# A recurrent attention with hash-routed experts: another order of TensorE's groups in a tick, readers of the scores swapped, decay checks and last rows moved

## Chip, cores and metric

The kernel runs on one core of a Trainium2 chip. The metric is device time in microseconds (us). A run gives one time; the profile comes from one execution of its own, whose time is given beside its span.

## What is computed

A state of 40x40 per batch and head is updated for 768 time steps (RWKV-7), in 32 independent batch-head pairs; each of the 3072 output rows (4 batches x 768 steps, 8 heads x 40 = 320 wide) then goes through one of 8 experts, chosen by a hash of its token id.

```python
for t in range(S):                      # B, H, S, D = 4, 8, 768, 40
    y[:, :, t] = einsum('bhd,bhde->bhe', rt, state)
    Sa = einsum('bhde,bhe->bhd', state, at)
    state = state * wt[:, :, None, :] - einsum('bhd,bhe->bhde', Sa, bt)
    state = state + einsum('bhd,bhe->bhde', vt, kt)
...
expert_idx = token_ids * 2654435761 % 8
out[mask] = maximum(x[mask] @ w1[e], 0) @ w2[e]      # 320 -> 1024 -> 320
```

## The kernel before

**Attention.** The 768 steps are cut into 12 chunks of 64 and the 4 batches into 2 pairs: 24 tiles (`NU`), each with 2 batches x 8 heads. Inside a chunk the recurrence becomes products of 64x64 matrices per head, with running products of the decays multiplied into a, b, k and out of r and y. A tile passes through these groups of matmuls on TensorE (PSUM tile in brackets):

- `at_t` (t_ps, L472) and `z` (z_ps, L437): transposes of the scaled a (`at`) and of the scaled b and k (`z`), copied out by ScalarE; `at` and `z` are made by VectorE (L422, L424).
- `a` (a_ps): the scores of a with k and b. VectorE masks the k part into `mk` (L455); ScalarE copies the b part into `pk` (L463, L465) and `no` (L466). VectorE and ScalarE read the same PSUM tile, one after the other, in the order in which the program has them.
- After four tiles VectorE inverts their 32x32 blocks: a transpose `nb` (L494), 31 pairs of `outer` and `ub` (L503, L506) spread over 3.2 ticks, and two transposes `ut`, `ug` (L514, L515).
- `x` and `u` (x_ps, u_ps): the rest of the inverse `um` from those blocks, by way of `xi` (ScalarE, L533, L536, L546).
- `r0` and `r1` (both into r1_ps): a times the state, then mk times v; ScalarE copies the sum into `r1` (L606).
- `c` (c_ps and nc_ps): C, in two layouts, copied by ScalarE into `c_t` (L625, one copy per head parity) and into `x` (L629). Between the 40 columns of one head and the next, `x`, `z` and other ring buffers hold zeroed gaps up to 64.
- `v_t`, `r_t` (v_ps, t_ps), `rc` (rc_ps): products of r with C and v, masked by VectorE into `mr` (L642).
- `s` (s_ps): the next state, `st` (VectorE, L660); `sd` (sd_ps): its transposes.
- `y` (y_ps): the output, scaled by VectorE into `xs` (L675) and stored to `x_rows` in HBM by POOL (L679).

These groups are put into "ticks". Tile u enters at tick u with `at_t`, `z`, `a`; its `x`, `u`, `r0`, `r_t`, `v_t` come at tick u+7, its `r1`, `c`, `rc`, `s` at u+8 (`LAG` = 8), its `y` and `sd` at u+9. So ticks 0 to 7 hold only the first groups, ticks 8 to 23 all of them, ticks 24 to 32 only the later ones. Inside a tick the order is that of the list `STEPS` (L273), each group at the fraction index/14; work without a step (loads, the pairs of outer and ub, the decays, the routing) has ticks of its own. The whole list, sorted by tick, is issued in that order on TensorE, VectorE, ScalarE and POOL (`manual_schedule`), and each engine works through its own in order. SP's queue is placed by the framework.

The PSUM tiles of two banks (`two_banks`, L203) share three buffers, so each group waits for the readers of an earlier one. `at_t`, `r_t`, `x`, `u`, `s` use another pool of two single banks.

**Decays.** Six rounds (`decays`, L292), each for two chunks, load w (L311), check with two Relu activations that all decays lie in 0.65 to 1.5 (L318, sums into `wbad`), and form running products on VectorE: `pb` (L323, L330), `qb` (L335), and so on to two stores `p_rows`, `q_rows` by SP (L303), which POOL reads back as `pl`, `ql` (L409, L410). If a check fails, slow loops at the end redo the work; with these inputs they do not run.

**Experts.** For each of 8 experts: indirect gathers of its rows by POOL (L865), transposes and copies (`columns_of`), `up` (L891, L896: two batches of four PSUM banks, Relu alternating between ScalarE and VectorE), and `down` (L909) in tiles of 128 rows, copied out by ScalarE (L913) and scattered by POOL (L914). The weights of expert 0 come early; those of 1 and 2 by POOL, the others by SP.

Of the kernel before, what the change touches and what calls it, by code (L numbers as in the profile page):

```python
# [43 lines left out]
def kernel(  # L44
# [13 lines left out]
    nc = tc.nc  # L58
# [43 lines left out]
    nc.vector.memset(ones[:], 1.0)  # L102


    wbad = route.tile([P, 4 * S * B * H // (C * P)], F32)


    FH = F // 2
# [60 lines left out]
        return t  # L169

    at_r, r_r = (ring(n, 2, [P, HP, P], gaps) for n in ("at", "r"))
    x_r = ring("x", 3, [P, 2, HP, P], gaps2)
    z_r = ring("z", LAG + 2, [P, 2, HP, R], gap)

# [95 lines left out]
    plan = []  # L270


    STEPS = ["r1", "v_t", "at_t", "z", "c", "y", "r_t", "sd", "a", "rc", "r0", "x", "s", "u"]  # L273

    def at_tick(tick, step=None, order=0):
        if step is not None:
# [5 lines left out]
        return add  # L282

    rounds = [dict() for _ in range(NR)]
    lim = hold.tile([P, 2], F32, name="lim")
    nc.vector.memset(lim[:, 0:1], LO)
    nc.vector.memset(lim[:, 1:2], -HI)
    SEG = 4
    HC = C // 2
    SL = HC // SEG  # L290
# [1 line left out]
    def decays(ri, t0, span, t_f, span_f):  # L292

        x = rounds[ri]
        todo, then = [], []

        def segs(t):
            return t[:, 0:HC * D].rearrange("p (s t e) -> p s t e", s=SEG, e=D)


        def store(i, src):
            for y in range(2 * RN):
                nc.sync.dma_start(pq_dram[ri][i][y * HC:(y + 1) * HC].rearrange("t bh e -> bh t e"),  # L303
                                  src[y * BH:(y + 1) * BH].rearrange("p (t e) -> p t e", e=D))

        @at_tick(t0 - 1.0)
        def _():
            x["qb"] = qb = early.tile([P, (HC + 1) * D], F32, tag="qb", name="qb")
            for y in range(2 * RN):
                src = w.rearrange("b h (n t) e -> (b h) n (t e)", t=HC)[:, ri * 2 * RN + y]  # L310
                nc.sync.dma_start(qb[y * BH:(y + 1) * BH, 0:HC * D], src)  # L311

        @todo.append
        def _():
            x["pb"] = pb = early.tile([P, (HC + 1) * D], F32, tag="pb", name="pb")[:, 0:HC * D]

            for i, (sign, at) in enumerate(((-1.0, LO), (1.0, HI))):
                nc.scalar.activation(pb, x["qb"][:, 0:HC * D], AF.Relu, bias=lim[:, i:i + 1], scale=sign,  # L318
                                     accum_out=wbad[:, 2 * ri + i:2 * ri + i + 1])

        @todo.append
        def _():
            nc.vector.memset(segs(x["pb"])[:, :, 0, :], 1.0)  # L323


        for i in range(1, SL):
            @todo.append
            def _(i=i):
                p = segs(x["pb"])
                nc.vector.tensor_tensor(p[:, :, i], p[:, :, i - 1], segs(x["qb"])[:, :, i - 1], op=OP.mult)  # L330
        for i in range(SL - 2, -1, -1):
            @todo.append
            def _(i=i):
                q = segs(x["qb"])
                nc.vector.tensor_tensor(q[:, :, i], q[:, :, i], q[:, :, i + 1], op=OP.mult)  # L335

        @todo.append
        def _():

            q = segs(x["qb"])  # L340
            x["own"] = own = work.tile([P, SEG, D], F32, tag="own", name="own", bufs=1)
            nc.vector.tensor_copy(own[:, SEG - 1], q[:, SEG - 1, 0])
            for s in range(SEG - 2, -1, -1):
                nc.vector.tensor_tensor(own[:, s], q[:, s, 0], own[:, s + 1], op=OP.mult)  # L344

        @then.append
        def _():
            x["f_ps"] = p = bank([P, D], "f_ps")
            nc.tensor.matmul(p, lhsT=partner[:], rhs=x["own"][:, 0], start=True, stop=True)  # L349

        @then.append
        def _():

            x["ends"] = ends = work.tile([P, SEG + 1, D], F32, tag="ends", name="ends", bufs=1)
            nc.vector.tensor_scalar(ends[:, SEG], x.pop("f_ps"), second[:, 0:1], None, op0=OP.add)
            nc.vector.tensor_tensor(ends[:, 0:SEG], x["own"][:],
                                    ends[:, SEG].unsqueeze(1).to_broadcast([P, SEG, D]), op=OP.mult)
            x["rends"] = rends = work.tile([P, SEG, D], F32, tag="rends", name="rends", bufs=1)
            nc.vector.reciprocal(rends[:], ends[:, 0:SEG])

        @then.append
        def _():

            p = segs(x["pb"])
            nc.vector.tensor_tensor(p, p, x["rends"][:].unsqueeze(2).to_broadcast([P, SEG, SL, D]), op=OP.mult)
            store(0, x["pb"])

        @then.append
        def _():
            q = segs(x["qb"])  # L370
            nc.vector.tensor_tensor(q, q, x["ends"][:, 1:].unsqueeze(2).to_broadcast([P, SEG, SL, D]),
                                    op=OP.mult)
            nc.vector.tensor_copy(x["qb"][:, HC * D:], x["ends"][:, SEG])
            store(1, x["qb"][:, D:])

        @then.append
        def _():

            p = bank([P, P], "en_ps")
            nc.tensor.transpose(p[0:D], x["ends"][:, 0], ident[:])  # L380
            t = pend_r(ri)
            for par in range(2):
                for rn in range(RN):
                    src = p[0:D, rn * 2 * BH:rn * 2 * BH + BH].rearrange("p (b hp two) -> p two hp b", hp=HP, two=2)
                    nc.scalar.copy(t[half40(par), :, rn, :], src[:, par])

        for i, f in enumerate(todo):
            at_tick(t0 + span * i / len(todo), order=8)(f)
        for i, f in enumerate(then):
            at_tick(t_f + span_f * i / len(then), order=8)(f)  # L390
# [4 lines left out]
    def tile_a(u):  # L395
# [17 lines left out]
            load(lambda be, rows: by_head(kb[:, be], rows), b, 2 * g, n * C)  # L413
            load(lambda be, rows: by_head(kb[:, be], rows), k, 2 * g, n * C, crossed=True)

        @at_tick(u - 0.6)
        def _():
            x["at"], x["z"] = at_r(u), z_r(u)

            def view(t):  # L420
                return t.rearrange("p (hp two e) -> p hp two e", hp=HP, two=2)
            nc.vector.scalar_tensor_tensor(wide(x["at"]), by_head(x["a"]), -1.0, by_head(x["p"]), op0=OP.mult, op1=OP.mult)  # L422
            for be in range(2):
                nc.vector.tensor_tensor(heads(x["z"][:, be]), view(x["kb"][:, be]), view(x["q"][:, be]), op=OP.mult)  # L424
# [17 lines left out]
        def _():  # L442
            gi, ti = divmod(u, GRP)
            p = two_banks("a_ps")
            for kb in range(2):
                order = ("hq", "al", "be", "par") if kb == 0 else ("hq", "be", "al", "par")
                for par, be, hp in heads_by(*order):
# [3 lines left out]
                       x["at_t"][half40(par), hp, be, :])  # L451
            scores = p[:].rearrange("p two (kb hp t) -> p two kb hp t", kb=2, t=C)
            of_b = scores[:, :, 1]
            x["mk"] = mk = work.tile([P, 2, HP, C], F32, tag="mk", name="mk", bufs=LAG)
            nc.vector.tensor_tensor(mk[:], scores[:, :, 0], after[:].unsqueeze(1).unsqueeze(1).to_broadcast([P, 2, HP, C]),  # L455
                                    op=OP.mult)

            if ti == 0:
                groups[gi]["pk"] = (early.tile([P, GRP * H * BLK], F32, tag="pk", name="pk")[:]
# [4 lines left out]
            for i in range(2):  # L464
                nc.scalar.copy(pk[low(i)], of_b[low(i), :, :, BLK:C])  # L465
            nc.scalar.copy(no[:], of_b[:, :, :, BLK:C])  # L466

    def turn(t, src):

# [113 lines left out]
    def tile_b(u, t0):  # L583
# [14 lines left out]
        def _():  # L598
            p = x.pop("r1_ps")

            for par, _, hp in heads_by("hq", "par", "al"):
                c0 = hp % HQ * 2 * D
                mm(p[half(al(hp)), par, c0:c0 + 2 * D], x["mk"][:, par, hp, :], x["x"][:, :, hp, par * C:par * C + D],
                   start=False)
            x["r1"] = r1 = work.tile([P, 2, HQ, 2, D], F32, tag="r1", name="r1")
            nc.scalar.copy(r1[:].rearrange("p two q b e -> p two (q b e)"), p[:, :, 0:HP * D])  # L606

        @at_tick(t0, "c")
        def _():
# [3 lines left out]
            for par, be, hp in heads_by("hq", "be", "al", "par"):  # L613
                h, a = hx(par, be, hp), al(hp)
                c0 = (be * HQ + hp % HQ) * C
                mm(p[half40(par), a, c0:c0 + C], r1[half(a), par, hp % HQ, be, :], um[half(a), h, :])
            if not last:
                q = two_banks("nc_ps")
                for par, be, hp in heads_by("hq", "par", "al", "be"):
                    h, a = hx(par, be, hp), al(hp)  # L620
                    c0 = (hp % HQ * 2 + par) * D
                    mm(q[half(be), a, c0:c0 + D], um[half(a), h, :], r1[half(a), par, hp % HQ, be, :])
            x["c_t"] = ct = work.tile([P, 2, HP, C], F32, tag="c_t", name="c_t", bufs=1)
            for par in range(2):
                nc.scalar.copy(ct[half40(par)].rearrange("p b (a q) t -> p a b (q t)", a=2),  # L625
                               p[half40(par), :, 0:HP * C].rearrange("p a (b x) -> p a b x", b=2))
            if not last:
                for be in range(2):
                    nc.scalar.copy(x["x"][half(be), be].rearrange("p (a q) (two e) -> p a (q two) e", a=2, two=2)[:, :, :, 0:D],  # L629
# [33 lines left out]
        def _():  # L663
# [12 lines left out]
                                    by_parity(x["py"]), op=OP.mult)  # L676
            for be in range(2):
                r0 = (2 * g + be) * S + n * C
                nc.gpsimd.dma_start(x_rows[r0:r0 + C, :], xs[half(be), :])  # L679

        if not last:
            @at_tick(t0 + 1, "sd")
# [266 lines left out]
    def columns_of(e, xgs):  # L949
# [11 lines left out]
            nc.vector.tensor_copy(xt[:, :, TPE * P:], others[0][:])  # L961
        return xt

    others = [None]
    with tc.manual_schedule(engines={ET.PE, ET.DVE, ET.Activation, ET.Pool}):
        xt = columns_of(0, rows_of(0))
        weights(1, moe_w1[1], moe_w2[1], nc.gpsimd.dma_start)
        for e in range(E):
            xgs = rows_of(e + 1) if e + 1 < E else None
            if e == 0:  # L970
                weights(2, moe_w1[2], moe_w2[2], nc.gpsimd.dma_start)
            ht = mwork.tile([P, FP, SLOTS], F32, tag="ht", name="ht")
            up(xt, w1s[e], ht, SLOTS)
            if xgs is None:
                rest()
            else:
                xt = columns_of(e + 1, xgs)
# [119 lines left out]
```

## Time and profile before

| what | us |
|---|---|
| median of 3 runs | 800.42 (799.39 to 804.31) |
| the profiled execution | 798.8 |
| its span, first to last instruction | 797.0 |
| mean granted clock of TensorE | 0.853 of full speed |
| TensorE busy | 630.0 (79%) |
| VectorE busy | 373.5 (47%) |
| ScalarE busy | 281.7 (35%) |
| POOL busy | 227.7 (29%) |

Busy times are those of instructions alone, without what issues DMAs. Line numbers are those of the kernel before. "Idle before" in a row is the engine's own idle time ahead of that instruction, and the arrow names what ended it.

### The profile page before, as it was taken

How to read it: one execution, taken by the hardware profiler on the slowest of the kernel's cores; microseconds unless marked ns; L12 is line 12 of the kernel's file. 1: busy time of each engine (PE TensorE's matmuls, PEld its weight loads, DVE VectorE, ACT ScalarE, POOL GpSimd, SP SyncE). 2: the span in 40 equal slices, each digit the busy share in tenths (PEclk: the TensorE clock that was granted, in tenths of full speed). 3: DMA queues.
4: the chain of work that ended last, by engine and by line, in shares of the span. 5: the costliest groups of instructions: out<-in, count | busy, mean ns of one | idle time of the engine just before them, and what ended most of it. 6: DMA issues, size and time to landing. Idle time of an engine off the chain costs nothing.

```text
span 797.0 us, 25924 instructions
## 1 busy us (share of the span) xinstructions
PE 630.0 (79%) x11272; PEld 466.4 (59%) x11272; DVE 373.5 (47%) x925; ACT 281.7 (35%) x630; POOL 227.7 (29%) x381
## 2 busy tenths in 40 slices
PE   0025356788979788887997989569999999999995
PEld 0024345677867677776876777536565565664653
DVE  7062899977865796445647823122112022120210
ACT  2024325566554664554665565101101011100110
POOL 3222134123343453343332322171220311312101
PEclk9996655688676996886889999569999999999998
DMA  5939696574699587766343432282234125323000
GB/s 99 168 75 182 107 186 129 102 152 93 100 135 134 92 134 120 104 129 110 62 57 71 94 78 47 84 244 86 54 108 134 58 91 175 103 84 103 25 4 25
DMA packets 204918, 82.43 MB, mean 103 GB/s; under 512 B 186622, under 2 KB 195839, under 8 KB 204800
## 3 DMA queue, kind: packets, MB, share of 16 engines
q1 hardware_dynamic: 193088, 47.27, 31.6%
q0 software_dynamic: 11712, 33.46, 18.2%
q8 instruction: 90, 1.47, 0.8%
q14 instruction: 28, 0.23, 0.1%
HBM read 64.92 MB, written 16.42 MB: 102 GB/s over the span
## 4 chain that ended last, share of the span: by engine, by line
PE 55%; issue 17%; DVE 13%; ACT 5%; DMA 4%; SPq 3%; POOL 2%; POOLq 0%; DVEq 0%; ACTq 0%
PE dn_ps L909 9%; PE up_ps L891 9%; PE y_ps L247 5%; PE s_ps L247 4%; PE r_ps L247 4%; PE rc_ps L247 3%; PE t_ps L472 3%; PE a_ps L247 2%; PE u_ps L247 2%; PE z_ps L437 2%; PE up_ps L896 2%; PE sd_ps L687 2%; PE x_ps L247 2%; DVE outer L503 2%; DVE ub L506 2%
## 5 line engine op out<-in xcount | busy, mean ns | idle before, releaser
L899 DVE TENSOR_SCALAR ht<-up_ps 128x448 f32<-128x448 f32 x32 | 20.0, 625 | 196.1 <-PE up_ps L896 130.2
L909 PE MATMUL dn_ps<-w,ht 128*128 128x320 f32 (+1 forms) x448 | 109.5, 433 | 0.0
L909 PEld LDWEIGHTS dn_ps<-w,ht 128*128 128x128 f32 (+1 forms) x448 | 72.0, 177 | 32.1 <-issue 1.3
L891 PE MATMUL up_ps<-xt,w 128*128 128x448 f32 x224 | 87.5, 544 | 0.0
L914 POOL DMA_INDIRECT out_dram<-o,idx_all x28 | 27.6, 987 | 197.9 <-ACT o L913 179.8
L891 PEld LDWEIGHTS up_ps<-xt,w 128*128 128x128 f32 x224 | 41.7, 190 | 43.1 <-issue 37.9
L506 DVE TENSOR_TENSOR ub<-ub,outer 128x31 f32<-128x31 f32 (+15 forms) x186 | 63.8, 343 | 6.4
L901 ACT ACTIVATE ht<-up_ps 128x448 f32<-128x448 f32 x32 | 17.4, 545 | 136.1 <-PE up_ps L896 101.7
L679 POOL DMA_DIRECT2D x_rows<-xs x48 | 25.4, 534 | 138.0 <-DVE xs L675 62.1
L503 DVE TENSOR_TENSOR outer<-ub,nb 128x31 f32<-128x31 f32 (+15 forms) x186 | 62.7, 337 | 3.2
L913 ACT COPY o<-dn_ps 128x320 f32<-128x320 f32 x28 | 11.9, 426 | 119.4 <-PE dn_ps L909 119.4
L247 PE MATMUL a_ps<-at_t,z_t 40*64 40x64 f32 x1536 | 37.6, 250 | 20.4 <-ACT z_t L439 13.2
L558 POOL MEMSET x<- 64x512 f32 x48 | 25.0, 520 | 94.2 <-PE s_ps L247 92.9
L247 PEld LDWEIGHTS a_ps<-at_t,z_t 40*64 40x64 f32 x1536 | 32.5, 158 | 27.9 <-ACT z_t L439 17.1
L409 POOL DMA_DIRECT2D pl<-p_rows x48 | 25.6, 534 | 78.2 <-DVE at L422 52.0
L349 PE MATMUL f_ps<-own,partner 128*128 128x40 f32 x12 | 3.8, 404 | 53.6 <-DVE own L344 53.4
L675 DVE TENSOR_TENSOR xs<-y_ps,py 128x320 f32<-128x320 f32 x24 | 11.8, 491 | 70.7 <-PE y_ps L247 64.9
L437 PE MATMUL z_ps<-ident,z 128*104 128x128 f32 x192 | 39.3, 373 | 1.2 <-DVE z L424 1.2
L463 ACT COPY pk<-a_ps 128x256 f32<-128x256 f32 x24 | 8.9, 373 | 82.6 <-DVE mk L455 78.9
L472 PE MATMUL t_ps<-ident,at 128*104 128x128 f32 x96 | 23.9, 398 | 16.3 <-DVE at L422 16.2
L437 PEld LDWEIGHTS z_ps<-ident,z 128*104 128x104 f32 x192 | 34.5, 186 | 2.4 <-issue 1.2
L349 PEld LDWEIGHTS f_ps<-own,partner 128*128 128x128 f32 x12 | 2.9, 290 | 54.6 <-DVE own L344 53.9
(179 smaller groups left out, 1302.2 us busy)
## 6 DMA issues: line engine op xcount, KB each, us to landing
ql<-q_rows POOLq DMA_DIRECT2D x48, 160.0 KB
w<-in_moe_w_dram SPq DMA_DIRECT2D x10, 640.0 KB
w<-in_moe_w_dram SPq DMA_DIRECT2D x10, 512.0 KB
qb<-in_w_dram SPq DMA_DIRECT2D x24, 160.0 KB
al<-in_a_dram SPq DMA_DIRECT2D x48, 80.0 KB
kb<-in_b_dram SPq DMA_DIRECT2D x48, 80.0 KB
kb<-in_k_dram SPq DMA_DIRECT2D x48, 80.0 KB
r<-in_r_dram SPq DMA_DIRECT2D x48, 80.0 KB
```

The costliest lines, as they stand in the source:

```text
L247: nc.tensor.matmul(out_, lhsT=lhsT, rhs=rhs, start=start, stop=stop, skip_group_check=True)
L409: nc.gpsimd.dma_start(pl[half(be)], of_batches(p_rows, 2 * g + be, 1))
L437: nc.tensor.transpose(p[0:R, be, hp * P:(hp + 1) * P], x["z"][:, be, hp, :], ident[:])
L472: nc.tensor.transpose(p[0:R, hp, :], src[:, hp, 0:R], ident[:])
L503: nc.vector.tensor_tensor(tv, ub[:, 0:j + 1, j:j + 1].to_broadcast([P, j + 1, m]), nb[:, j, j + 1:].unsqueeze(1).to_broadcast([P, j + 1, m ...
L506: nc.vector.tensor_tensor(o, o, tv, op=OP.add)
L558: nc.gpsimd.memset(x["x"][half(be), be], 0.0)
L679: nc.gpsimd.dma_start(x_rows[r0:r0 + C, :], xs[half(be), :])
L891: nc.tensor.matmul(p[:], lhsT=w1[c][:, (f0 + i) * P:(f0 + i + 1) * P], rhs=xt[:, c, 0:n], start=(c == 0), stop=False)
L899: nc.vector.tensor_scalar(ht[:, f0 + i, 0:n], p[:], 0.0, None, op0=OP.max)
L909: nc.tensor.matmul(p[i * m:(i + 1) * m], lhsT=ht[:, f, c0:c0 + m], rhs=w2[f // (FP // 2)][:, f % (FP // 2), :], start=(f == 0), stop=(f == ...
L914: st = nc.gpsimd.indirect_dma_start(out=out[:], out_offset=bass.IndirectOffsetOnAxis(ap=idx, axis=0), in_=o[0:m], in_offset=None, bounds_c ...
```

## The change

1. `STEPS` has another order. `c` comes before `z`; `x` between `z` and `y`; `s` before `a`; `rc` at the end of the tick, behind `r0` and `u`.
2. `mk` is made after ScalarE's copies of the scores, so ScalarE reads the scores first and VectorE second.
3. `r1` becomes a ring of two buffers with zeroed gaps from 40 to 64 columns per head, so that C fills whole halves of the partitions and is copied out in one instruction in place of two.
4. The two checks leave the rounds of the decays. `check_decays` reads all of w again in four parts of 128x1920 during experts 1 to 4, by POOL, and checks each part on ScalarE behind that expert's `up`.
5. The rows of the last two tiles are stored by SP, not by POOL.
6. The gathers for experts 0 and 1 come ahead of the loads of the weights of experts 1 and 2.
7. `at` and `z` are made at u-0.5 in place of u-0.6.

```diff
-    wbad = route.tile([P, 4 * S * B * H // (C * P)], F32)
+    WP = 4
+    wbad = route.tile([P, 2 * WP], F32)
+    lim = route.tile([P, 2], F32)
+    nc.vector.memset(lim[:, 0:1], LO)
+    nc.vector.memset(lim[:, 1:2], -HI)
...
+    r1_r = ring("r1", 2, [P, 2, HP, C], gap)
...
-    STEPS = ["r1", "v_t", "at_t", "z", "c", "y", "r_t", "sd", "a", "rc", "r0", "x", "s", "u"]
+    STEPS = ["r1", "v_t", "at_t", "c", "z", "x", "y", "r_t", "sd", "s", "a", "r0", "u", "rc"]
...
             x["pb"] = pb = early.tile([P, (HC + 1) * D], F32, tag="pb", name="pb")[:, 0:HC * D]
-
-            for i, (sign, at) in enumerate(((-1.0, LO), (1.0, HI))):
-                nc.scalar.activation(pb, x["qb"][:, 0:HC * D], AF.Relu, bias=lim[:, i:i + 1], scale=sign,
-                                     accum_out=wbad[:, 2 * ri + i:2 * ri + i + 1])
-
-        @todo.append
-        def _():
             nc.vector.memset(segs(x["pb"])[:, :, 0, :], 1.0)
...
-        @at_tick(u - 0.6)
+        @at_tick(u - 0.5)
...
             of_b = scores[:, :, 1]
-            x["mk"] = mk = work.tile([P, 2, HP, C], F32, tag="mk", name="mk", bufs=LAG)
-            nc.vector.tensor_tensor(mk[:], scores[:, :, 0], after[:].unsqueeze(1).unsqueeze(1).to_broadcast([P, 2, HP, C]),
-                                    op=OP.mult)
...
             nc.scalar.copy(no[:], of_b[:, :, :, BLK:C])
+            x["mk"] = mk = work.tile([P, 2, HP, C], F32, tag="mk", name="mk", bufs=LAG)
+            nc.vector.tensor_tensor(mk[:], scores[:, :, 0], after[:].unsqueeze(1).unsqueeze(1).to_broadcast([P, 2, HP, C]),
+                                    op=OP.mult)
...
-            x["r1"] = r1 = work.tile([P, 2, HQ, 2, D], F32, tag="r1", name="r1")
-            nc.scalar.copy(r1[:].rearrange("p two q b e -> p two (q b e)"), p[:, :, 0:HP * D])
+            x["r1"] = r1 = r1_r(u)
+            nc.scalar.copy(r1[:, :, :, 0:D], p[:, :, 0:HP * D].rearrange("p two (x e) -> p two x e", e=D))
...
-                mm(p[half40(par), a, c0:c0 + C], r1[half(a), par, hp % HQ, be, :], um[half(a), h, :])
+                mm(p[half(par), a, c0:c0 + C], r1[half(a), par, hp % HQ * 2 + be, :], um[half(a), h, :])
...
-                    mm(q[half(be), a, c0:c0 + D], um[half(a), h, :], r1[half(a), par, hp % HQ, be, :])
+                    mm(q[half(be), a, c0:c0 + D], um[half(a), h, :], r1[half(a), par, hp % HQ * 2 + be, 0:D])
...
-            for par in range(2):
-                nc.scalar.copy(ct[half40(par)].rearrange("p b (a q) t -> p a b (q t)", a=2),
-                               p[half40(par), :, 0:HP * C].rearrange("p a (b x) -> p a b x", b=2))
+            nc.scalar.copy(ct[:].rearrange("p b (a q) t -> p a b (q t)", a=2),
+                           p[:, :, 0:HP * C].rearrange("p a (b x) -> p a b x", b=2))
...
-                nc.gpsimd.dma_start(x_rows[r0:r0 + C, :], xs[half(be), :])
+
+                dma = nc.sync.dma_start if u >= NU - 2 else nc.gpsimd.dma_start
+                dma(x_rows[r0:r0 + C, :], xs[half(be), :])
...
+    def check_decays(i):
+        wr = w.rearrange("b h s e -> (b h s e)").rearrange("(p n x) -> n p x", p=P, n=WP)[i]
+        t = mwork.tile([P, wr.shape[1]], F32, tag="wr", name="wr")
+        nc.gpsimd.dma_start(t[:], wr)
+        o = mwork.tile([P, wr.shape[1]], F32, tag="wo", name="wo")
+        for j, sign in enumerate((-1.0, 1.0)):
+            nc.scalar.activation(o[:], t[:], AF.Relu, bias=lim[:, j:j + 1], scale=sign,
+                                 accum_out=wbad[:, 2 * i + j:2 * i + j + 1])
...
-        xt = columns_of(0, rows_of(0))
-        weights(1, moe_w1[1], moe_w2[1], nc.gpsimd.dma_start)
+        xgs = rows_of(0)
+        xt = columns_of(0, xgs)
         for e in range(E):
             xgs = rows_of(e + 1) if e + 1 < E else None
             if e == 0:
-                weights(2, moe_w1[2], moe_w2[2], nc.gpsimd.dma_start)
+                for i in range(1, 3):
+                    weights(i, moe_w1[i], moe_w2[i], nc.gpsimd.dma_start)
...
             up(xt, w1s[e], ht, SLOTS)
+            if 0 < e <= WP:
+                check_decays(e - 1)
```

## The prediction

> **What bounds the kernel now.** I read the stages first. The columns are the stretch, its length, then busy us (and instructions) of TensorE (PE), weight loads (PEld), VectorE (DVE), ScalarE (ACT) and GpSimd (POOL), then the granted clock, the DMA share and GB/s.
>
> ```profile
> 0.00:62.00 62.00, 7.77 (x94) 6.05 (x94) 29.47 (x76) 11.32 (x25) 14.64 (x49) 1.00 0.64 120
> 62.00:154.00 92.00, 50.70 (x968) 42.61 (x968) 71.38 (x178) 37.88 (x89) 25.20 (x50) 0.59 0.74 135
> 154.00:430.90 276.90, 238.59 (x6799) 205.91 (x6800) 185.84 (x449) 159.67 (x361) 105.16 (x174) 0.79 0.68 110
> 430.90:511.00 80.10, 70.94 (x2444) 61.65 (x2436) 37.63 (x79) 43.45 (x97) 19.19 (x39) 0.90 0.27 61
> 511.00:528.40 17.40, 3.58 (x12) 1.79 (x12) 4.01 (x16) 0.00 (x0) 9.78 (x13) 0.50 0.63 180
> 528.40:797.00 268.60, 258.43 (x970) 148.37 (x970) 45.16 (x130) 29.36 (x60) 53.78 (x57) 0.98 0.28 90
> ```
>
> Start (0 to 62), ramp (ticks 0 to 7, VectorE busiest), full ticks (8 to 23), last ticks, a gap, the experts (TensorE 96% busy). The mask product mr starts at 152.72 in tick 8 and at 419.17 in tick 23, so a full tick takes (419.17-152.72)/15 = 17.8 us. TensorE's groups of one tick at full clock, by their starts between 409 and 426 us, sum to about 11.2 us; the rest is half-rate clock and idle. Then TensorE's waits in 154 to 425 (total us, times, longest):
>
> ```profile
> PE x_ps L247 <- issue: 7.3, 4, 2.5
> PE a_ps L247 <- issue: 7.1, 3, 4.3
> ...
> PE u_ps L247 <- ACT xi L533: 4.0, 3, 3.3
> ...
> PE nc_ps L247 <- ACT v_t L581: 3.1, 2, 1.6
> ...
> PE y_ps L247 <- ACT z_t L439: 1.6, 2, 0.8
> ```
>
> Some 28 us is "issue" (TensorE waited for nothing that the profile shows), which I leave as it is; only 10.4 us is waits for ScalarE (these three, 1.4 for um, 0.3 for r1).
>
> **Start: checks leave ScalarE.** In the start, VectorE's chain of decays stands behind the two Relu checks of the same tile:
>
> ```profile
> 7.11 1.36 ACT L318 ACTIVATE pb<-qb,lim 128x1280 f32<-128x1280 f32 x1
> ...
> 10.14 0.19 DVE L323 MEMSET pb<- 128x160 f32 x1 [3.16 <-ACT pb L318]
> ...
> 42.18 0.19 DVE L323 MEMSET pb<- 128x160 f32 x1 [20.33 <-ACT pb L318]
> ```
>
> Without them the first chain starts when VectorE is free, at 6.98 instead of 10.14: -3.1. The second waits for its own load (landed 39.1), which waits for the stores of the first (-3.1 again, same shift) and then no longer for 1.36+0.19+1.36+0.19: another -2.9. The chain of waits runs through both to 62 us, so -6.0 together (-3 if the second load's landing doesn't move).
>
> **Ramp.** VectorE is busy 71.38 of 92 us and loses 4.7 us there waiting for the checks of round 2; mk (mask of the scores) held ScalarE's copies back for 44.9 us in all, which the swap of readers ends. I take -4 (from -8 to 0: mk may in turn wait for the copies, 1.6 us each).
>
> **Full ticks: what is removed.** All but the 0.3, 10.1 us: v_t no longer waits behind checks, z_t has c, nc and x between it and y, and xi is no longer behind a late mk. C in one copy takes ScalarE 0.59 (nearest row v_t, 104x512) instead of 2x0.58; c's weights grow from 40 to 64 columns, whose nearest row, nc with 64, has the same pitch (0.43 us); the copy of r1 in heads of 40 is taken as 0.43, as before. ScalarE is at 58% and hides these.
>
> **Full ticks: what is added.** rc moves to the tick's end, and mk is now behind ScalarE's copies, with rows of "outer"/"ub" and the 32x32 transposes between mk and mr. In the changed program nc or z, whichever gets rc's banks, waits for mr; before, z or c waited with 4.6 us of work between rc and it. Today's order, with mk first and its copies next:
>
> ```profile
> 415.30 0.69 DVE L455 TENSOR_TENSOR mk<-a_ps,after 128x512 f32<-128x512 f32 x1 [1.93 <-PE a_ps L247]
> ...
> 416.02 0.37 ACT L463 COPY pk<-a_ps 128x256 f32<-128x256 f32 x1 [1.01 <-DVE mk L455]
> ...
> 417.19 0.37 ACT L466 COPY no<-a_ps 128x256 f32<-128x256 f32 x1
> 417.20 2.09 DVE L494 STREAM_TRANSPOSE nb<-pk 128x1024 f32<-128x1024 f32 x1 [1.21 <-ACT pk L465]
> ...
> 419.17 1.19 DVE L642 TENSOR_TENSOR mr<-rc_ps,after 128x1024 f32<-128x1024 f32 x1
> ```
>
> From a's end TensorE reaches nc after r0 0.65, u 0.62, rc 0.98, r1 0.70, v 0.43, at 0.38, c 0.43 = 4.2 us, z after 4.65; I use 4.5, at clock 0.79 5.7. mr ends after 1.48 (four copies) + 0.69 (mk) + 1.22 (mr) + 0.3 (handovers) = 3.7 plus what stands between mk and mr. Ordinary tick: three pairs of 0.7 (outer 0.34, ub 0.34): 5.8, a wait of 0.1 (1.3 at full clock). Tick with nb: 2.06 and two pairs at 0.45: 6.65, a wait of 1.0 (2.1). Tick with ut and ug, which now stand ahead of mr and not behind it: 1.97+2.07+0.9: 8.6, a wait of 2.9 (4.1). Of the 16 ticks 8 are ordinary, 4 and 4 the others: 0.8+4+11.6 = 16.4 (35 at full clock). An issue stall in that stretch takes the wait's place: it is 4.5/11.2 of the tick's work, so 11 of the 28 us lie there; I let half (5) count. Added 11.4, removed 10.1: **+1**, with ends of -26 (all absorbed, and clock 0.79 to 0.84 on 238.6 us of busy time: 14) and +27 (35 less most of the 10.1). Behind nc or z wait x, y and all of TensorE's tick, then xs and st on VectorE.
>
> **What a wait does to the clock.** Here a row and a rule differ.
>
> ```profile
> 400.00:405.00 5.00, 3.61 (x92) 2.60 (x91) 3.40 (x4) 2.74 (x8) 0.96 (x3) 0.76 0.48 41
> 405.00:410.00 5.00, 5.00 (x70) 4.43 (x68) 2.48 (x3) 2.35 (x6) 2.49 (x4) 0.55 0.22 36
> ```
>
> In the first stretch TensorE idles 1.4 us; in the second it is busy throughout at half clock. The Trainium skill (TensorE: Matmul & The Clock Gate, "Why this matters for your kernels") says that gaps of over about 3 us drop the clock. By the rule only the 4.1 us waits of ut and ug could cost clock; by the row each wait over about 1 us costs some 2 us more (about 4 us at half rate). The row decides. By it the added waits (8 over 1 us) cost 16 and the removed ones (4 over 1 us: 3.3, 1.6, 1.5, 1.4) give back 8: +8; but issue stalls drop the clock in most of these ticks anyway, so I take +2 and keep +8 for the range.
>
> **Last ticks.** Waits for xi and mr (2.6 us) go; tick 26 has ut and ug ahead of mr, +1: -1.6. c still waits for r1's copy.
>
> **Gap: last rows by SyncE, gathers first.** POOL issues the last rows behind a weight load of SP, and four gathers follow:
>
> ```profile
> 510.21 0.94 SPq L121 DMA_DIRECT2D w<-in_moe_w_dram  x2
> 510.90 1.04 POOL L679 DMA_DIRECT2D x_rows<-xs  x2 [4.16 <-DVE xs L675]
> ...
> 518.11 1.02 POOL L865 DMA_INDIRECT xg<-x_rows,src_all  x1 [6.17 <-issue]
> ...
> 527.14 0.90 PE L874 MATMUL xg_ps<-ident,xg 128*128 128x128 f32 x3 [2.58 <-DMA xg<-x_rows,src_all]
> ```
>
> The 1.28 MB of w move at about 390 GB/s until 516, and the rows land at 516.5 with them; the rows of the tick before, alone, were through within 2 us. In SP's queue they now stand ahead of w: landing near 513 and gathers 3.5 earlier. The fourth gather took 5.2 us to land against 3.0 for the first, as the weights of expert 1 join it; with seven gathers first, -1.5. Sum **-5** (-1 if SP's issue is late, -7 at most). SP's load of w shifts by under 1 us and is for a later expert; expert 1's weights keep their place near 523 (seven gathers of 1.28 from 514.6) and are needed at 560.
>
> **Experts.** Four loads of 983 KB (w's 390 GB/s gives 2.5 us), issued by POOL behind gathers, and 2 x (1.36x1.5+0.19) = 4.5 us on ScalarE (estimate from the 128x1280 row). They lie between the last Relu of "up" and the first copy of "down", 5.5 us later (1.13 transposes, 4.3 for one tile of down, a third of 12.92); cover gone, at most 4.5 each, so 0 (to +3). Two memsets and lim at the start lie on idle POOL and VectorE; at and z, half a tick ahead, stay just behind xs: 0.
>
> **Sum.** -6.0 -4 +1 +2 -1.6 -5 = -13.6 on the profiled execution's 798.8 (span 797.0 and 1.8 around it): 785.2. The median of the runs is 1.6 above that execution: **786.8**.
>
> **Rivals.**
> - The full ticks gain: issue stalls absorb the new waits and the clock rises to 0.84. -26 in place of +3: 758; with half of it, 771. For it: only 10.4 us of waits need vanish, and those in dip-prone ticks. Against: 28 us of issue stays.
> - Little is gained: the start stays bound by loads (DMA 0.64) and the ramp by VectorE; -3, 0, +3, -1.6, -3: 796. For it: VectorE is at 78% in the ramp with waits for loads (7.0 for al). Against: the chain passes through the checks by name.
> - Slower, by one mechanism: mr behind mk, the pairs and ut/ug, with TensorE at its door at full clock. 35 us of waits, less 10.1, plus 8 of clock: +33 and with the other terms 816; it decides from the point where a full tick loses over 1.0 us net (the other terms' 16.6 spread over 16 ticks). For it: 4.2 us against 5.8 to 8.6. Against: at the clock that is granted most ordinary ticks hide it.
>
> **How the numbers follow.** Forecast 0.46 (own range 777 to 797), gain in the ticks 0.2, little 0.17, slower 0.17. Within 1% (792.4 to 808.4; about what this measurement can tell from no change) lie 0.07 of the first, 0.14 of the third and 0.04 of the last: 0.25. Faster: 0.39+0.2+0.03 = 0.62; slower 0.13. The range leaves out the outer part of gain and slower: 763 to 808.
>
> **What would show it.** Right: VectorE's first decay product near 7.0 and the second chain near 36; mr within 6 us of a's end in ordinary ticks, nc or z waiting for mr mainly in ticks with ut and nb; rows landed by 514 and "up" starting some 5 us after what the shifted ticks give. Wrong: a full tick away from 17 to 18.7 us, or a stage clock away from 0.76 to 0.82; then the place of mr tells which rival it is.

## The result and the profile after

The changed kernel took 782.86 us (median of 4 runs, 779.79 to 792.26) beside 802.23 for the kernel before on the same chip: a ratio of 0.975 (0.970 to 0.979). Measured twice more, each time beside the kernel before, it gave 796.12 (ratio 0.990, 0.981 to 0.999) and 791.32 (beside 800.5, without an interval). So the gain is 1 to 2.5%, and the forecast of 786.8 lies among the three medians. The profiled execution of the change was one of its slower ones (792.26, some 10 us over the other three runs), so I read two further profiles of the same kernel beside it, and no difference below about 1% between two kernels is taken as settled here.

The stages of the changed kernel, in the columns of the table of before. The first two cuts are those of before less 7.2 us, by which mr of tick 8 moved; the others lie within 0.5 us of the same events:

```profile
0.00:54.80 54.80, 7.53 (x84) 5.95 (x85) 28.95 (x75) 4.02 (x13) 15.04 (x51) 1.00 0.73 126
54.80:146.80 92.00, 60.93 (x1064) 50.13 (x1066) 74.61 (x185) 37.44 (x92) 25.13 (x50) 1.00 0.80 147
146.80:429.20 282.40, 239.78 (x6754) 205.63 (x6746) 185.66 (x443) 143.41 (x333) 105.78 (x176) 0.81 0.65 106
429.20:508.80 79.60, 70.73 (x2418) 61.27 (x2410) 37.34 (x79) 37.62 (x86) 17.18 (x35) 0.91 0.27 60
508.80:521.50 12.70, 3.47 (x13) 2.52 (x14) 4.43 (x18) 0.00 (x0) 7.91 (x10) 0.50 0.71 203
521.50:790.00 268.50, 258.36 (x970) 148.07 (x969) 44.79 (x128) 44.74 (x76) 56.89 (x64) 0.98 0.33 107
```

The full ticks begin 7 us earlier, and the gap is nearly 5 us shorter; the experts are as long as they were, although ScalarE does 15 us more there; the full ticks are 5 to 6 us longer, at a clock a little higher. By landmarks (mr of tick 8 starts, mr of tick 23 starts, the last xs ends, "up" starts), with the two further profiles of the change:

| us | before | after | again | third |
|---|---|---|---|---|
| mr of tick 8 starts (start and ramp) | 152.72 | 145.48 | 145.55 | 146.64 |
| one full tick (mr 8 to mr 23, over 15) | 17.76 | 18.14 | 18.26 | 18.23 |
| last ticks (mr 23 to the last xs) | 91.4 | 90.4 | 92.5 | 94.9 |
| gap (last xs to "up") | 17.8 | 13.1 | 13.1 | 13.1 |
| span | 797.0 | 790.1 | 793.9 | 797.1 |

Start and gap keep their gain in every profile; what is lost again is lost in the ticks.

VectorE's two chains of decays, from the timeline of the changed kernel (start, duration, engine, line, idle before and what ended it):

```profile
7.42 2.48 DVE L325 TENSOR_TENSOR pb<-pb,qb 128x160 f32<-128x160 f32 x7
...
36.62 2.48 DVE L325 TENSOR_TENSOR pb<-pb,qb 128x160 f32<-128x160 f32 x7 [12.64 <-DMA qb<-in_w_dram]
```

The first product was due near 7.0 and came at 7.42; the second chain was due near 36 and came at 36.62, and what it waits for is now its load, not ScalarE. The first scores (a_ps) started at 57.87 before and 52.10 after: 5.8 us.

The gap, VectorE's first copy behind the rows before the change, and then the timeline of the changed kernel:

```profile
516.67 0.18 DVE L992 COPY selq<-ident 128x32 f32<-128x32 f32 x1 [6.06 <-DMA x_rows<-xs]
```

```profile
507.51 0.49 DVE L669 TENSOR_TENSOR xs<-y_ps,py 128x320 f32<-128x320 f32 x1 [1.38 <-PE y_ps L252]
509.37 1.01 SPq L125 DMA_DIRECT2D w<-in_moe_w_dram  x2
510.85 0.18 DVE L1000 COPY selq<-ident 128x32 f32<-128x32 f32 x1 [2.85 <-DMA x_rows<-xs]
511.76 1.02 POOL L861 DMA_INDIRECT xg<-x_rows,src_all  x1 [12.69 <-DVE selq L1002]
...
521.08 1.86 PE L887 MATMUL up_ps<-xt,w_0pk 128*128 128x448 f32 x2 [0.39 <-DVE xt L876]
```

VectorE's copy of `selq` waits for the rows: they landed 2.85 us after xs, where it had been 6.06 behind the load of w. SP issues w after them, at 509.37. The first gather is issued at 511.76; between the last xs and "up" lie 13.08 us in place of 17.82. Of the 4.7 us, 3.2 are the rows (6.06 to 2.85) and 1.5 come behind `selq`, where the gathers now stand ahead of the weights.

TensorE's waits in 145 to 425 us of the changed kernel (total us, times, longest):

```profile
PE rc_ps L252 <- issue: 16.1, 10, 3.5
...
PE nc_ps L252 <- DVE mr L636: 4.0, 2, 3.2
...
PE v_ps L575 <- ACT r L601: 1.6, 3, 0.5
```

The waits for v_t, z_t, xi and um are gone here: ScalarE is down from 10.6 to 1.6 us in that stage (3.2 and 1.7 in the two further profiles). The new wait of nc for mr is there, 4.0 us in all (5.1 with z), where the added waits had been sized at 16.4. "Issue" did not shrink: from mr of tick 8 to mr of tick 23 it was 27.9 us before, and 36.0, 32.9 and 35.5 in the three profiles of the change. It moved, from x, a and s to rc and u.

### The profile page after: what moved, and what is told of

Same layout as the page of the kernel before. It is cut to its first block, busy times and chain, and to the rows that moved or that the text cites. A ratio compares the mean times of both kernels' runs of the same rounds, so it can differ in the third digit from the quotient of the medians.

```text
span 790.1 us, 25829 instructions
## 1 busy us (share of the span) xinstructions
PE 640.8 (81%) x11272; PEld 473.6 (60%) x11272; DVE 375.8 (48%) x925; ACT 267.2 (34%) x598; POOL 227.9 (29%) x383
## 4 chain that ended last, share of the span: by engine, by line
PE 50%; issue 24%; DVE 12%; DMA 4%; POOL 4%; SPq 3%; ACT 1%; POOLq 0%; DVEq 0%; another core or an unknown queue 0%
PE y_ps L252 6%; PE up_ps L887 6%; PE dn_ps L905 5%; PE s_ps L252 4%; PE t_ps L467 4%; PE r_ps L252 4%; PE rc_ps L252 3%; PE z_ps L432 3%; PE sd_ps L683 3%; PE x_ps L252 2%; DMA qb<-in_w_dram 2%; PE c_ps L252 2%; PE a_ps L252 2%; POOL out_dram L910 2%; PE nc_ps L252 2%
## 5 line engine op out<-in xcount | busy, mean ns | idle before, releaser
L675 POOL DMA_DIRECT2D x_rows<-xs x44 | 23.3, 535 | 200.0 <-DVE xs L669 163.2
L467 PE MATMUL t_ps<-ident,at 128*104 128x128 f32 x96 | 24.0, 399 | 16.4 <-DVE at L417 14.3
L252 PE MATMUL y_ps<-z,mr 128*64 128x40 f32 x768 | 33.2, 250 | 2.8 <-issue 1.9
L636 DVE TENSOR_TENSOR mr<-rc_ps,after 128x1024 f32<-128x1024 f32 x24 | 29.1, 1214 | 11.3 <-PE rc_ps L252 11.2
L432 PEld LDWEIGHTS z_ps<-ident,z 128*104 128x104 f32 x192 | 31.6, 178 | 3.8 <-issue 1.3
L861 POOL DMA_INDIRECT xg<-x_rows,src_all x28 | 27.0, 963 | 20.9 <-DVE selq L1002 12.7
```

Source lines behind the costliest of these rows:

```text
L252: nc.tensor.matmul(out_, lhsT=lhsT, rhs=rhs, start=start, stop=stop, skip_group_check=True)
L432: nc.tensor.transpose(p[0:R, be, hp * P:(hp + 1) * P], x["z"][:, be, hp, :], ident[:])
L467: nc.tensor.transpose(p[0:R, hp, :], src[:, hp, 0:R], ident[:])
L636: nc.vector.tensor_tensor(t[:].rearrange("p two h t -> p (two h) t"), p[:].rearrange("p two (h t) -> p (two h) t", t=C), after[:].unsqueez ...
L861: nc.gpsimd.indirect_dma_start(out=xg[0:m], out_offset=None, in_=x_rows[:], in_offset=bass.IndirectOffsetOnAxis(ap=idx, axis=0))
```

## The experiments

Two questions. Does each part bring what its step of the sum says? And is VectorE's order at the end of a tick (mk, the pairs, the transposes, then mr) what the ticks lose by, as the third rival has it with a larger price, or is it a cost that "issue" stalls and half clock hide? The intervals are those of the ratio to the kernel before on the same chip.

**The change again, and its three thirds.** `after_again` is the changed kernel. The others are the kernel before with some parts of the change: `checks_alone` has part 4, `gap_alone` parts 5 and 6, `tick_alone` parts 1, 2, 3 and 7. Their diffs are the lines of those parts in the diff above; in short:

```diff
 checks_alone
-                nc.scalar.activation(pb, x["qb"][:, 0:HC * D], AF.Relu, ...
+            if 0 < e <= WP:
+                check_decays(e - 1)
 gap_alone
+                dma = nc.sync.dma_start if u >= NU - 2 else nc.gpsimd.dma_start
+        xgs = rows_of(0)
+        xt = columns_of(0, xgs)
 tick_alone
+    STEPS = ["r1", "v_t", "at_t", "c", "z", "x", "y", "r_t", "sd", "s", "a", "r0", "u", "rc"]
+            x["r1"] = r1 = r1_r(u)
```

> The changed kernel itself, for a second profile; nothing in it differs. The first profile has a full tick of (417.63-145.48)/15 = 18.1 us against 17.8 before, and its time is about 10 us over the other runs. Theory A (start -6 to -7, gap -5, full ticks near nothing): ratio to before 0.975 to 0.985, a full tick of 17.5 to 18.0. Rival B (the ticks gained too): a full tick under 17.4, and the ratio at 0.975 or below.

> The kernel before with part 4 alone: the two checks out of the decays' rounds, beside the experts. Theory A: the chain of decays starts 3 us earlier in round 0 and 6 in round 1, so mr of tick 8 comes 6 to 10 us earlier (152.7 before) and the whole gains 6 to 13 us (0.984 to 0.993). Rival B (the start is bound by loads): mr of tick 8 earlier by under 3 us, whole 0.995 to 1.0. Rival C (the checks also cost the full ticks, in ticks 11 and 15): a gain of over 13.

> The kernel before with parts 5 and 6 alone: last rows by SP, gathers ahead of the weights. Theory A: from the end of the last xs (510.6) to the first up (528.4), 17.8 us before, shrinks to about 13, and the whole gains 5 us (0.994). Rival B (SP's issue or the weights' later start give it back): 16 to 17 us, or expert 1 waits for its weights, and 0.998 to 1.0.

> The kernel before with parts 1, 2, 3 and 7: the order in a tick, readers swapped, C in one copy; checks still in the rounds, gap as before. Theory A: removed and added waits are about equal; full tick 17.3 to 18.2 us, whole 0.993 to 1.006, with waits of nc or z for mr of 5 to 15 us that the kernel before has not. Rival B (the order is where the gain lies): 0.985 or below, full tick under 17.2. Rival C (mr late costs clock as well): above 1.01, full tick above 18.5.

| kernel | us | ratio | mr 8 starts | full tick | gap |
|---|---|---|---|---|---|
| after_again | 796.12 | 0.990 (0.981 to 0.999) | 145.55 | 18.26 | 13.1 |
| checks_alone | 794.74 | 0.988 (0.983 to 0.992) | 145.47 | 17.85 | 17.7 |
| gap_alone | 799.51 | 0.992 (0.987 to 0.996) | 151.83 | 17.85 | 13.0 |
| tick_alone | 809.36 | 1.006 (1.002 to 1.010) | 155.65 | 18.78 | 18.5 |

The kernel before took 805.96 here. By these ratios the parts are worth -10, -7 and +5 us. The checks alone move mr of tick 8 as far as the whole change does, and the rows with the gathers alone close the gap as far. What concerns the ticks costs 1.8 to 8.2 us. `tick_alone` missed its Theory A in two points: its full tick is 18.78 us, above the 17.3 to 18.2 expected, and TensorE's waits for mr come to 0.6 us from tick 8 to tick 23 (and 3.6 in ticks 23 to 26) where 5 to 15 were expected, so its loss is not made of waits that the profile names. The product of the three ratios is 0.985, between the two ratios of the whole change, so no large interplay is needed. With the checks alone, the waits for ScalarE in 146 to 430 us fall from 10.6 to 5.3 us (that for v_t goes, those for xi, um and z_t stay), and the full tick does not get shorter for it.

**The old ticks, the old order, and later transposes.** `checks_and_gap` joins parts 4, 5 and 6 and keeps the old ticks. `old_order` is the whole change with the old list, so that mr stands ahead of ut and ug again while the copies, the ring and the readers stay changed. `transposes_late` is the change with the transposes a little later in the list, which puts nb, ut and ug behind mr:

```diff
 old_order
+    STEPS = ["r1", "v_t", "at_t", "z", "c", "y", "r_t", "sd", "a", "rc", "r0", "x", "s", "u"]
 transposes_late
-        group_i(gi, t0 + 0.05, t0 + 0.1, t0 + 3.2)
+        group_i(gi, t0 + 0.25, t0 + 0.3, t0 + 3.3)
```

> The changed kernel once more, as the yardstick of the three others on the same chip. The two looks so far gave ratios of 0.975 and 0.990 to the kernel before; 0.975 to 0.992 is expected, with a full tick of 17.8 to 18.3 us.

> The kernel before with parts 4, 5 and 6 (checks beside the experts, last rows by SP, gathers first), its ticks as before. Theory A (the gain lies outside the ticks, and the ticks of the change lose a little): the product of the parts measured alone, 0.9875 x 0.9915 = 0.979, so 2 to 10 us below the changed kernel. Rival B (the ticks of the change gain once the checks are gone from ScalarE): above the changed kernel by 3 us or more.

> The changed kernel with the old order of the groups in a tick (part 1 undone alone). Theory A (the order is what costs the ticks, by waits for mr and by a dense run of small matmuls at the tick's end): 2 to 8 us below the changed kernel, no waits of nc or z for mr, the issue stalls no longer gathered at u and rc. Rival B (the swap of readers or the single copy of C costs): no change, within 2 us. Rival C (the order is what gains): 4 us or more above.

> The changed kernel with nb, ut and ug put behind mr in VectorE's order (the inversion of a group a fifth of a tick later). Theory A as first stated (waits for mr in the ticks with ut and nb cost some 12 us): 5 to 12 us below the changed kernel and no wait for mr over 1.5 us. Rival (these waits replace issue stalls, or are as small as the 4 to 5 us in the profiles): 0 to 4 us below.

| kernel | us | ratio | full tick |
|---|---|---|---|
| after_third | 791.32 (773.76 to 799.25) | - | 18.23 |
| checks_and_gap | 792.38 | 0.983 (0.974 to 0.992) | 18.13 |
| old_order | 789.51 | 0.981 (0.972 to 0.989) | 17.81 |
| transposes_late | 774.29 | 0.966 (0.955 to 0.976) | 16.59 |

The first three cannot be told apart: without the new ticks, or with only TensorE's old order, the kernel is where the whole change is. Their profiles also show how loose the full tick of one execution is: `checks_and_gap` has the ticks of the kernel before and 18.13 in place of 17.76. The median of `transposes_late` stands apart, 2% below theirs, but one of the four runs of the change took 773.76, inside its range (767.01 to 783.06); the runs further down settle it.

The tick with ut and ug in the changed kernel, from its timeline; a's last matmul ends at 179.00:

```profile
182.24 1.95 DVE L509 STREAM_TRANSPOSE ut<-ub 128x1024 f32<-128x1024 f32 x1
...
184.05 1.85 DVE L510 STREAM_TRANSPOSE ug<-ub 128x1024 f32<-128x1024 f32 x1
185.79 1.18 DVE L636 TENSOR_TENSOR mr<-rc_ps,after 128x1024 f32<-128x1024 f32 x1
...
187.03 0.68 PE L252 MATMUL nc_ps<-r,um 64*64 64x40 f32 x32 [3.17 <-DVE mr L636]
```

rc was complete at 181.16 (start 180.51, 0.65 long), and mr ran at 185.79: it had stood behind ut and ug, and nc waited 3.17 us behind mr. The same tick with the transposes behind mr; a's last matmul ends at 168.94:

```profile
172.63 1.22 DVE L636 TENSOR_TENSOR mr<-rc_ps,after 128x1024 f32<-128x1024 f32 x1
...
174.04 1.93 DVE L509 STREAM_TRANSPOSE ut<-ub 128x1024 f32<-128x1024 f32 x1
...
174.55 0.20 PE L252 MATMUL nc_ps<-r,um 64*64 64x40 f32 x1
```

mr ends 4.9 us after a (8.0 before the edit), and nc starts without a wait for it; c, just ahead of it, has an issue stall of 0.99 us instead.

**Does it repeat, and which transposes is it?** `late_again` is the kernel of `transposes_late` once more. `late_mask_first` also takes mk ahead of the copies again (part 2 undone). `only_ut_late` moves ut and ug alone (the 31 pairs are spread over 3.2 ticks by it in place of 3.1). `tick_late_alone` is `tick_alone` with the late transposes.

```diff
 late_mask_first
+            x["mk"] = mk = work.tile([P, 2, HP, C], F32, tag="mk", name="mk", bufs=LAG)
...
             nc.scalar.copy(pk, of_b[:, :, :, 0:BLK])
 only_ut_late
-        group_i(gi, t0 + 0.05, t0 + 0.1, t0 + 3.2)
+        group_i(gi, t0 + 0.05, t0 + 0.1, t0 + 3.3)
 tick_late_alone
-        group_i(gi, t0 + 0.05, t0 + 0.1, t0 + 3.2)
+        group_i(gi, t0 + 0.25, t0 + 0.3, t0 + 3.3)
```

> The changed kernel with nb, ut and ug behind mr, once more: its first look was 0.966 of the kernel before (0.955 to 0.976), on a chip where the changed kernel's own runs spread from 774 to 799. Theory A (the wait of nc and z for mr behind the transposes is what the new order pays): 0.96 to 0.975 again, a full tick of 16.4 to 17.2 us. Rival (the first look was luck of the clock): 0.98 to 0.99, as the changed kernel, with a full tick near 18.

> The kernel with late transposes, and mk made ahead of ScalarE's copies again (part 2 undone). Theory A (mr waits behind mk, so an earlier mk can only help mr, but a late VectorE holds ScalarE's copies back): within 4 us of the late kernel. Rival B (the swap of readers is what gains in the ticks): 5 us or more above it, with waits of u for xi again. Rival C (the swap costs): 4 us or more below.

> The changed kernel with ut and ug alone behind mr, nb left ahead of it. Theory A (two transposes ahead of mr cost 4 us each time, nb 2): two thirds or more of the late kernel's gain, 3 to 7 us above the late kernel. Rival (nb is what costs): about the changed kernel's time.

> The kernel before with parts 1, 2, 3 and 7 and the transposes late; checks and gap as before. With the transposes ahead of mr these parts gave 1.006. Theory A: the new order without the late mr takes waits for ScalarE away and adds none: 0.985 to 0.995, full tick 16.6 to 17.5 us. Rival (late transposes only help together with the checks' leaving): 0.998 or above.

| kernel | us | ratio | full tick | last ticks |
|---|---|---|---|---|
| late_again | 774.62 | 0.963 (0.956 to 0.971) | 17.97 | 84.5 |
| late_mask_first | 777.70 | 0.967 (0.960 to 0.974) | 17.67 | 89.0 |
| only_ut_late | 776.08 | 0.961 (0.952 to 0.970) | 17.43 | 86.3 |
| tick_late_alone | 792.68 | 0.989 (0.980 to 0.997) | 17.33 | 84.2 |

The gain repeats, though not the full tick of 16.4 to 17.2 us expected of `late_again` (17.97 in its profile). Moving ut and ug alone brings all of it to within 1.5 us, where a time 3 to 7 us above the late kernel had been expected; nb ahead of mr costs nothing that can be measured, and the swap of readers brings nothing that can be measured. For the ticks by themselves the same edit turns 1.006 into 0.989. The kernels with late ut and ug that also hold the checks and the rows take 774 to 778 us where the change takes 783 to 796.

This changes what is to be said of the new order. `old_order` has ut and ug behind mr, as the kernel before had them, and gains nothing over the change (789.51); the new order with ut and ug behind mr is 15 us below it. So the new order does gain, some 1 to 2%, and the change as it stands lost that again because the new order let ut and ug in ahead of mr. Parts 3 and 7 have no run of their own.

**Where it comes from.** Over the 16 ticks from 8 to 23 I took the time from a's end to the first nc. It is 8.31, 8.75 and 8.14 us in the mean in the three profiles of the change, and 7.28, 7.66, 7.80 and 7.66 in `transposes_late`, `late_again`, `late_mask_first` and `only_ut_late`. The means of the two groups, 8.40 and 7.60, differ by 0.80, over 16 ticks 13 us; the medians of the runs differ as much: the mean of the medians is 790.1 us for the three series of the change and 775.7 for the four late ones. In the profiles the spans differ by 18.8 us in the mean: 12 in the full ticks, 5 in the last ticks, 2 ahead of them. So most of it lies in that stretch, and in few ticks: its mean falls from 8.09 to 7.04 us in the ticks with ut and ug and from 8.65 to 6.94 in the ticks just behind those (with nb), but only from 8.43 to 8.21 in the 8 ordinary ones, which is within their scatter.

By parts, TensorE is busy for 5.86 us of the stretch in place of 6.26 (half clock makes the same work longer); waits that name mr go from 0.22 to 0.02, and issue stalls from 1.75 to 1.59. The named waits are thus the smaller part: from tick 8 to tick 23 they are 3.4 to 5.1 us in the three profiles of the change, and c, which waits for no mr, itself starts earlier after a (7.26 before, 6.62 after). Fewer stalls are not the reason either: from mr of tick 8 to mr of tick 23 the four late kernels have 27.7, 33.2, 30.7 and 37.2 us of them, the change 33 to 36.

What a wait for mr brings with it can be seen by itself in tick 26, which has ut and ug and where no issue stall stands beside the wait. The changed kernel, with three stretches around it in the columns of the stages:

```profile
455.10 1.89 DVE L510 STREAM_TRANSPOSE ug<-ub 128x1024 f32<-128x1024 f32 x1
456.88 1.18 DVE L636 TENSOR_TENSOR mr<-rc_ps,after 128x1024 f32<-128x1024 f32 x1
...
458.11 1.09 PE L252 MATMUL nc_ps<-r,um 64*64 64x40 f32 x32 [2.11 <-DVE mr L636]
```

```profile
452.00:456.00 4.00, 3.84 (x178) 3.31 (x169) 3.86 (x8) 1.67 (x4) 1.17 (x3) 1.00 1.00 213
456.00:460.00 4.00, 1.89 (x64) 1.81 (x64) 2.06 (x2) 1.24 (x3) 0.00 (x0) 0.68 0.34 110
460.00:464.00 4.00, 4.00 (x77) 3.71 (x73) 0.49 (x1) 1.82 (x5) 0.09 (x1) 0.50 0.04 6
```

The same tick in `only_ut_late`:

```profile
441.85 1.23 DVE L636 TENSOR_TENSOR mr<-rc_ps,after 128x1024 f32<-128x1024 f32 x1 [0.35 <-PE rc_ps L252]
442.99 1.94 DVE L509 STREAM_TRANSPOSE ut<-ub 128x1024 f32<-128x1024 f32 x1
```

```profile
443.00:447.00 4.00, 3.34 (x155) 3.13 (x156) 3.69 (x3) 2.89 (x7) 0.00 (x0) 1.00 0.30 112
447.00:451.00 4.00, 4.00 (x122) 3.39 (x118) 1.05 (x3) 2.06 (x5) 2.72 (x6) 1.00 0.56 148
```

The clock falls to half while TensorE waits and stays there for 10.2 us, with TensorE busy throughout behind the wait. The two further profiles of the change have the same wait of 2.11 us and then half clock for 6.8 us, `tick_alone` one of 2.2 us and, 2.4 us behind it, 3.4 us at half clock. The kernels with late ut and ug have neither: full clock for 12 us behind mr in all of them. From mr of tick 25 to mr of tick 27 the change takes 25.7, 26.8 and 27.1 us, the four late kernels 22.5 to 22.9. So this wait costs 3.7 us in the mean, 2.1 by itself and the rest behind it, net of pauses of 0.7 to 1.2 us that the late kernels have in its place. The longer wait of the tick shown further up (3.2 to 3.4 us) is likewise followed by half clock for 10.2 us in all three profiles, and in `transposes_late` the clock is 1.00 from 163.5 to 187 us. In the other ticks stalls and waits are mixed, and how much of the 13 us goes this way stays open.

## Why the prediction was right, and which steps of it were off

- **The number.** In part luck. By the first profile the span changed by -6.9 us, the sum of -5.8, -1.4, +5.7, -1.1, -4.7 and +0.4 for start, ramp, full ticks, last ticks, gap and experts, where -13.6 was forecast; by the medians the change is -19.4, -9.8 and -9.2. The terms of start and gap hold; ramp and ticks were 2.6 and 2.7 us too favourable, and the three medians of one kernel lie 13 us apart.
- **Start (-6.0).** Right in mechanism and size: 5.8 at the first scores, both chains within 0.7 us of the times named. The second half of it held because the load came earlier too; the chain now waits for that load.
- **Ramp (-4).** Too large: 94.85 us from the first scores to mr of tick 8 became 93.38, so -1.4, inside the range given (-8 to 0). VectorE was taken to lose 4.7 us to checks and mk to hold ScalarE; but VectorE is busy for 74.6 of the ramp's 92 us, more than before (71.4), and the swap of readers brings nothing: `checks_alone`, with mk first, reaches tick 8 at 145.47, as the whole change does.
- **What is removed in the ticks (-10.1).** The waits went (10.6 to 1.6), as said, but were worth little: `checks_alone` lost 5.3 us of them and its full ticks did not get shorter (17.85 against 17.76).
- **What is added (+16.4, less 5).** When mr ends was right: from a's end 5.9 to 7.8 us in the 8 ordinary ticks (median 6.25, forecast 5.8), 6.4 to 6.5 in three ticks with nb and 7.7 in the fourth (6.65), 8.0 to 8.3 in those with ut and ug (8.6). The step that failed is the other side: "I use 4.5, at clock 0.79 5.7". TensorE reached nc after 8.3 in the mean. Its busy time there, 6.03 us, is near the 5.7; the issue stalls are what was sized too small. "11 of the 28 us lie there; I let half (5) count" is 0.3 us a tick; they were 1.8 us a tick in this stretch, 29 us of the 36 over the 16 ticks. So most waits vanished behind them: 3.4 to 5.1 us remain of the 16.4. One is shown in full: 3.17 us, where 2.9 to 4.1 was given.
- **The ticks as a whole (+1 +2).** Small and positive was right: `tick_alone` says +5 (1.8 to 8.2), which also holds its part of the ramp and last ticks. But it is not made of waits as I had it: it goes with ut and ug, through the stretch ahead of nc, and it is the remainder of a gain of the new order (0.989 with late ut and ug) and a loss by them.
- **Clock (+2).** Not seen: 0.79 before; 0.82, 0.80 and 0.81 from mr 8 to mr 23 in the three profiles. But between the row and the rule the runs decide for the row: the wait of 2.11 us in tick 26, shorter than the 3 us of the rule, was followed by half clock in all three profiles of the change, and the wait of 2.2 us in `tick_alone` too. What came on top of the wait, 1.6 us in the mean, is near the 2 us taken from the row. The mean did not move because few such waits were left: from tick 8 to tick 23 one or two over 1 us in each profile of the change.
- **Last ticks (-1.6).** Not to be told from nothing: -1.1, +1.0 and +3.5 in three profiles. The +1 for tick 26 is there as a wait of nc for mr of 2.1 us, with half clock behind it; the late kernels take 3.7 us less there.
- **Gap (-5).** Right: -4.7, and `gap_alone` gives -7 (3 to 10) for the whole. Both halves fit: 3.2 for the rows where 3.5 was named, 1.5 for the gathers. The rows landed at 510.85, 2.85 us after the end of xs; by 514 was named.
- **Experts (0).** Right: 268.6 and 269.1. The cover held: each pair of checks takes ScalarE 2x(1.89+0.19) = 4.2 us and no wait of TensorE was added there.

Of the rivals, "the full ticks gain" did not occur in the change; it does when ut and ug are behind mr (`tick_late_alone`, 0.980 to 0.997). The slower one, "mr behind mk, the pairs and ut/ug", names the right place and the right pair of transposes, at about a seventh of its price: +5 for +33, with 0.4 to 0.5 us lost per full tick where 1.0 would have decided it. "Little is gained" erred on start and gap, which kept all they promised.

## What to carry to other kernels

Work that a reorder gathers behind one late group is to be counted from both ends: when the buffer is released and when the next user really arrives, with the stalls and the clock of that stretch in the arrival, not only the sum of its instructions. On an in-order engine a long instruction that is needed next tick belongs behind the short one that releases a buffer: 3.9 us of transposes put behind a 1.2 us product, with no work saved, decided here whether the new order gained 15 us or nothing. When a list is reordered, look at what the other engines' lists now put in front of each short one: what the first engine gains can be lost there. A wait also has to be priced with the clock behind it: 2.1 us cost 3.7 here. Checks on the way of the first loads, and a last store queued behind a big load, are cheap to find in the chain of waits and give what they promise.

## What the runs showed that was not expected

- The stalls without a releaser are a fixed companion of the full ticks: 28 us before, 33 to 36 in the three profiles of the change and 28 to 37 in the late kernels. The traces show what they go with. The profile has a DMA queue named "instruction"; in the full ticks it moves 51 packets of 16 KB, one for some 265 of TensorE's matmuls and weight loads. Of the 272 stalls of over 0.5 us in the full ticks of all 14 profiles, 240 end 1.2 to 1.8 us after such a packet has landed; of matmuls drawn at random from those without a stall, 9 to 15% start so. So most of these stalls look like TensorE waiting for its next instructions. That is read from the timing alone; no run tests it, and in `after_again` 9 of 20 stalls and in `tick_alone` 8 of 20 do not fit.
- The granted clock that a profile shows holds only from its first clock record on. In the first profile of the change that is 140.0 us (57.9 in the profile before), and the 1.00 of its start and ramp is no measurement: the group of 64 matmuls that takes 1.16 us at full clock elsewhere took 2.46, as it does before the change where the clock is shown at 0.50. The same makes its mean clock of 0.908 too high (0.856 in the third profile).

```profile
95.22 2.46 PE L252 MATMUL a_ps<-at_t,z_t 40*64 40x64 f32 x64 [0.68 <-ACT z_t L434]
```

- One and the same kernel spreads by 3% on one core: the change took 773.8 to 799.6 us in all, and 773.8 to 799.3 in four runs side by side. One profile's stage, like one run, says little about a per cent.
